# Second experts without GpSimd: VectorE makes every lower half, and the weight sums of the second product end one step earlier

## The chip, the cores and the metric

One core of one Trainium2 chip runs the whole program. The metric is device time in microseconds (us): the median of three runs before the change is 1219.12 us (1217.57 to 1220.42).

## The reference, cut to what matters

Linear attention with a norm over each head, then a layer with a SiLU gate, then four weighted experts. The last part is what the change touches:

```python
p = domain_probs / (domain_probs.sum(-1, keepdims=True) + 1e-09)
for e in range(E):                                # N = 2304, D = 512, E = 4, F = 1024
    h = np.maximum(x @ w1[e], 0.0)
    out += p[:, e:e + 1] * (h @ w2[e])
```

## The kernel before, in words

**Number format.** Each float32 operand of a matmul is held as two rounded parts, an upper half and a lower half. `split` (L157) makes them: ScalarE copies the value into the rounded type (upper half, L159), then VectorE or GpSimd subtracts that copy from the value (lower half, L160). A product uses upper times upper, lower times upper and upper times lower, so three matmuls stand for one.

**First stage, to about 466 us.** Attention and the first layer, in an order that a table (`PROGRAM`) and a loop over units fix. Its last two units overlap with the opening of the second experts; `flush` (L831) adds their results into `acc` on VectorE, four instructions at a time (L839).

**Second experts, class `Second`, from about 466 us to the end.** The 2304 tokens are three tiles of 768 tokens (two halves of 384 each; the short words of the change call a tile a pair of halves). The four experts are taken as eight halves of 512 hidden columns. So there are 24 steps, step n being expert half n mod 8 on tile n div 8. In a step the first product (`first`, L256) takes seven sub-products of twelve matmuls, built from sums and differences of quarter blocks: with weights a11, a12, s2, s1, s3, s4, a22 and inputs b11, b21, t2, t1, t3, b22, t4. The results go through `keep` (ScalarE), `add` and `relu` (VectorE), become c11, c12, c22, c21, and `oph` splits them into hidden operands. The second product reads those: in the eight steps of tile 0 by `second` (L313, plain blocks, eight groups of twelve matmuls), in tiles 1 and 2 by `again` (L338, the seven sub-products, with hidden sums t1 to t4 from `sumh`). `gather` adds each result into `acc` on VectorE (L310).

**Weights.** In tile 0 the weights are loaded (`load1`, `load2`), split (`op1`, `op2`) and written split to DRAM (`put_away`, L218); tiles 1 and 2 read them back (`get`, L223). The sums s1 to s4 of the second product's weights are needed from step 8 on. They are made by VectorE (`sumw`, L202) in a loop of their own over the eight expert halves, split by `op2` and put away. `opx` splits the inputs of a tile (seven per tile), `sumx` (L233) makes t1 to t4 of the inputs.

**What sets the order.** `events` (L372) gives each call a slot; one slot is one sub-product of TensorE, a step has 15 slots (14 from step 9 on), and `self.start[n]` is the first slot of step n. The calls are sorted by slot and issued in that order. Every engine, and SP's queue that issues all these DMAs, takes its own instructions strictly in that order: an instruction that waits holds back all that stand behind it on its engine. So `put_away` in SP's queue waits for the lower half that it writes, and the loads behind it wait too. Calls at negative slots (`early`) are issued among the units of the first stage, the others after its last unit.

**GpSimd's part before.** `pool` (L379) goes as the engine of the lower half to: three of seven inputs of a tile (`opx`), all seven first weights of step 0 and three of seven in steps 1 to 7 (`op1`), three of four plain second weights in steps 0 to 7 (`op2`), and of the hidden operands c22 in step 0 and in steps 8 to 23, t3 and t4 in steps 8 to 23 (`oph`).

**PSUM.** Two accumulators per product, x and z, lie in two banks that swap roles each step (`bank`, L166). TensorE may write a bank again when `keep`, `add`, `relu` or `gather` has read it.

Of the kernel before, what the change touches and what calls it, by code (L numbers as in the profile page):

```python
# [80 lines left out]
class Second:  # L81
# [290 lines left out]
    def events(self):  # L372
# [3 lines left out]
        def put(slot, f, *a):  # L376
            ev.append((slot, len(ev), f, a))

        pool = self.nc.gpsimd  # L379
        for n in range(self.steps):  # L380
            t, q = divmod(n, E2)
            b0, after = self.start[n], self.start[n + 1]
            make = t == 0

            if q == 0:
                start_of_last = self.start[max(n - 1, 0)]
                at = [start_of_last + k for k in (2.2, 4, 8.2, 9.4)] + [b0 + k for k in (6.2, 3, 8.2)]

                of = {"t1": start_of_last + 7.2, "t2": start_of_last + 7.3, "t3": b0 + 5.5, "t4": b0 + 7.3}
                if t == 0:  # L390

                    at = [k - 27 for k in (0, 1, 3, 2, 5, 6, 4)]
                    of = {self.B[k]: (min(at[2:4]) - 0.2 if k == 3 else at[k] - 0.1) for k in (2, 3, 4, 6)}
                for k in range(7):
                    put(at[k], self.opx, t, k, pool if k in (1, 3, 5) and t == 0 or k in (0, 1, 5) and t else None)
                    if self.B[k][0] == "t":
                        put(of[self.B[k]], self.sumx, t, self.B[k])
                for k, name in ((3, "t1"), (6, "t2"), (6, "t4"), (4, "t3")):
                    put(max(at[2:4]) + 0.01 if k == 3 else at[k] + 0.01, self.t.pop, (t, name))

            lead = self.LEAD + (2.5, -2)[n] if n < 2 else self.LEAD
            for k in range(7):
                i = b0 + 1 + 2 * k
                put(i, self.first, n, k)
                if q == E2 - 1:
                    put(i + 0.01, self.x.pop, (t, k))
                if not make:
                    put(i - self.LEAD, self.get, n, 1, k)
                    continue
                if k == 2:  # L410
                    put(i - lead - (1.8 if n != 1 else 0.2), self.sumw, n, 1, "s1")
                    put(i - lead - (1.7 if n != 1 else 0.1), self.sumw, n, 1, "s2")
                if k in (4, 5):
                    put(i - lead - 1.7, self.sumw, n, 1, "s3" if k == 4 else "s4")
                put(i - lead, self.op1, n, k, pool if k in (1, 4, 6) or n == 0 else None)
                put(i - lead + 2, self.put_away, n, 1, k)
            if make:
                for k, (i, j) in enumerate(((1, 0), (1, 1), (0, 0), (0, 1))):
                    put(b0 - (self.LEAD + 5 if n else 35) + 0.5 * k, self.load1, n, i, j)
                for k, name in ((4, "a11"), (4, "a21"), (5, "a12"), (6, "a22"), (3, "s1"), (4, "s3"), (5, "s2"), (5, "s4")):  # L420
                    put(b0 + 1.01 + 2 * k - lead, self.raw.pop, (n, 1, name))
            put(b0 + 2.1, self.keep, n, "x", "c11")
            put(b0 + 4.1, self.add, n, "z", "c11")
            put(b0 + 6.1, self.keep, n, "x", "c12")
            put(b0 + 8.1, self.keep, n, "z", "c22")
            put(b0 + 10.1, self.add, n, "x", "c22")
            put(b0 + 12.1, self.add, n, "z", "c12")
            put(b0 + 12.2, self.ps.pop, (n, "z"))

            put(b0 + 4.3, self.relu, n, "c11")  # L430
            put(b0 + (5.3 if n else 6.15), self.oph, n, "c11")
            put(b0 + 10.3, self.relu, n, "c22")
            put(b0 + 10.5, self.oph, n, "c22", None if make and n else pool)
            put(b0 + 12.25, self.relu, n, "c12")
            put(b0 + 14.05, self.relu, n, "c21")
            put(b0 + 14.06, self.ps.pop, (n, "x"))
            if make:
                put(b0 + 12.5, self.oph, n, "c12")
                put(b0 + 14.1, self.oph, n, "c21")
                for i, name in ((5.4 if n else 6.2, "c11"), (12.6, "c22"), (12.6, "c12"), (14.2, "c21")):  # L440
                    put(b0 + i, self.f.pop, (n, name))

                for k, (i, j) in enumerate(((0, 0), (0, 1), (1, 0), (1, 1))):
                    at = b0 + ((7.2, 8.6, 10.2, 14.7) if n else (7.2, 8.6, 15.2, 17.7))[k]
                    put(at - 5.5, self.load2, n, i, j)
                    put(at, self.op2, n, f"a{i + 1}{j + 1}", pool if k != 1 else None)
                    put(at + 0.01, self.raw.pop, (n, 2, f"a{i + 1}{j + 1}"))
                    if k != 2:
                        put(at + 2.5, self.put_away, n, 2, (0, 1, None, 6)[k])
                for b in range(4):  # L450
                    for d in range(2):
                        put(after + 4 * b + 2 * d, self.second, n, b, d)
                    put(after + 4 * b + 3.2, self.gather, n, b, *self.BLOCKS[b])
                    put(after + 4 * b + 3.21, self.ps.pop, (n, b))
                for i in range(2):
                    for j in range(2):
                        put(after + (10.1, 14.1)[1 - j], self.h.pop, (n, f"b{i + 1}{j + 1}"))
                        put(after + (6.1, 14.1)[i], self.w2.pop, (n, f"a{i + 1}{j + 1}"))
            else:
                put(b0 + 12.3, self.sumh, n, "t1")  # L460
                put(b0 + 12.31, self.f.pop, (n, "c12"))
                put(b0 + 12.4, self.oph, n, "t1")
                put(b0 + 12.5, self.sumh, n, "t2")
                put(b0 + 12.51, self.f.pop, (n, "c22"))
                put(b0 + 12.52, self.f.pop, (n, "t1"))
                put(after + 1.11, self.oph, n, "t2")
                put(after + 1.12, self.sumh, n, "t3")
                put(after + 1.13, self.f.pop, (n, "c11"))
                put(after + 1.14, self.oph, n, "t3", pool)
                put(after + 1.15, self.f.pop, (n, "t3"))  # L470

                u = after + (1 if n < self.steps - 1 else 3)
                put(u + 0.16, self.sumh, n, "t4")
                put(u + 0.17, self.f.pop, (n, "t2"))
                put(after + 5.5, self.oph, n, "t4", pool)
                put(after + 5.51, self.f.pop, (n, "t4"))
                put(after + 3.3, self.oph, n, "c21")
                put(after + 3.31, self.f.pop, (n, "c21"))
                for m, k in enumerate(self.ORDER):
                    put(after + 2 * m, self.again, n, k)  # L480
                    put(after + 2 * m - self.LEAD, self.get, n, 2, k)
                for m, g in enumerate(self.GATHER):
                    last = n == self.steps - 1
                    if last and m == 6:
                        for d in range(2):
                            put(after + 2 * m + 0.45, self.gather, n, *g, d)
                    else:
                        put(after + 2 * m + (1.1 if m < 6 else 0.45), self.gather, n, *g)
                put(after + 11.2, self.ps.pop, (n, "oz"))
                put(after + 12.46, self.ps.pop, (n, "ox"))  # L490
            if n == E2:
                put(b0 + 2.0, self.change)
            if q % 2 == 0:
                put(b0 - 8 if n else 0, self.load_p, t, q // 2)
            else:
                put(b0 + 14.06, self.pb.pop, (t, q // 2))
            if n == self.steps - 1:
                parts = ((9.5, 1, 0), (11.5, 1, 1), (13, 0, 0), (16, 0, 1, (0,)), (16, 0, 1, (1,)))
                for b, (slot, j, i, *ds) in enumerate(parts):
                    put(after + slot, self.leave_last, j, i, b, *ds)  # L500
            elif q == E2 - 1:
                for k in range(PW // 256):
                    put(self.start[n + 3 + k] + 11.5, self.leave, n + 2 + k, t, 2 * k)

        for n in range(E2):
            a, b = self.start[2 * n] + (7 if n == 0 else 0), self.start[2 * n + 1] + (3 if n == 0 else 0)
            for k, (i, j) in enumerate(((1, 0), (1, 1), (0, 0), (0, 1))):
                put(a + 0.4 + 0.1 * k, self.load2, n, i, j, True)
            for at, name in ((a, "s1"), (a + 2, "s2"), (b, "s3"), (b + 2, "s4")):
# [467 lines left out]
```

## Time and profile before

| what | value |
|---|---|
| runs | 1217.57, 1219.12, 1220.42 us |
| the profiled execution | 1215.1 us, of which 1213.2 us are the span of the core |
| TensorE matmul busy | 1178.1 us (97%) |
| VectorE busy | 838.1 us (69%) |
| ScalarE busy | 459.7 us (38%) |
| GpSimd busy | 312.5 us (26%) |
| chain that ended last | TensorE 83%, VectorE 2%, ScalarE 1% of the span |

The profile's numbers are of one execution; its 1215.1 us are 4.0 us under the median of the runs. TensorE is called PE, VectorE DVE, ScalarE ACT, GpSimd POOL and SyncE SP in the rows. A row of the timeline is an instruction or several equal ones, with its start, its length, and in brackets how long its engine was idle before it and what released it. Busy time says where an engine worked, the idle time of TensorE what can be won.

### The profile page before, as it was taken

The numbers are of one execution on the slowest core, as the hardware profiler recorded it, in microseconds if no ns is written. First come the engines' busy times: TensorE is split into PE (matmuls) and PEld (weight loads), VectorE is DVE, ScalarE is ACT, GpSimd is POOL, SyncE is SP. The second block draws the span as 40 slices with busy tenths as digits, with TensorE's granted clock in tenths as the row PEclk, the third lists the DMA queues.
The fourth block names the chain that finished last, engine by engine and source line by source line (L and its number), as shares of the span: only waits on it lengthen the run. The fifth ranks groups of instructions, "written<-read, shape, count | busy, mean of one in ns | idle before, by whom it ended". The sixth has DMA issues, their size and how long they took to land.

```text
span 1213.2 us, 17113 instructions
## 1 busy us (share of the span) xinstructions
PE 1178.1 (97%) x6513; PEld 1105.0 (91%) x6513; DVE 838.1 (69%) x1081; ACT 459.7 (38%) x726; POOL 312.5 (26%) x220
## 2 busy tenths in 40 slices
PE   6899999999999999999999999999999899999997
PEld 5777798888888889999999999999999899999997
DVE  4986554655564456877777867788888876666775
ACT  4555543343333243544444433333333332333222
POOL 3553442311310013522222311111113211111112
PEclk9999999999999999999999999999999999999999
DMA  9613121200200007799878677999998878888763
GB/s 327 216 57 114 35 70 35 71 18 1 97 27 1 1 1 238 274 358 323 315 271 309 237 281 281 317 308 338 307 323 285 290 241 249 277 266 277 248 203 120
DMA packets 94854, 242.91 MB, mean 200 GB/s; under 512 B 11244, under 2 KB 42420, under 8 KB 94772
## 3 DMA queue, kind: packets, MB, share of 16 engines
q1 hardware_dynamic: 92756, 238.63, 57.9%
q10 hardware_dynamic: 2016, 3.18, 0.7%
q8 instruction: 52, 0.85, 0.3%
q14 instruction: 30, 0.25, 0.1%
HBM read 178.30 MB, written 63.48 MB: 199 GB/s over the span
## 4 chain that ended last, share of the span: by engine, by line
PE 83%; DVE 2%; issue 1%; ACT 1%; DMA 0%; DVEq 0%; ACTq 0%
PE ps_x L251 16%; PE a L827 13%; PE p_h L789 12%; PE ps_z L251 12%; PE ps_o L332 11%; PE ps_ox L251 10%; PE ps_oz L251 8%; DVE f L286 0%; PE ps_t L350 0%; DVE f L269 0%; DMA w<-w_dram 0%; DVE s L202 0%; DVE t L292 0%; DVE acc L310 0%; ACT hid L159 0%
## 5 line engine op out<-in xcount | busy, mean ns | idle before, releaser
L251 PE MATMUL ps_x<-x,w 128*128 128x384 f32 x1152 | 215.8, 335 | 1.9 <-ACT x L159 1.9
L251 PEld LDWEIGHTS ps_x<-x,w 128*128 128x128 f32 x1152 | 201.4, 188 | 2.3 <-ACT x L159 2.2
L251 PE MATMUL ps_z<-x,w 128*128 128x384 f32 x864 | 163.6, 337 | 2.1 <-DVE f L286 2.1
L251 PEld LDWEIGHTS ps_z<-x,w 128*128 128x128 f32 x864 | 152.4, 189 | 2.9 <-DVE f L286 2.5
L159 ACT ACTIVATE hid<-f 128x768 fp32r<-128x768 f32 x80 | 67.6, 845 | 211.3 <-DVE f L286 211.3
L251 PE MATMUL ps_ox<-hid,w 128*128 128x384 f32 x768 | 145.0, 337 | 2.1 <-issue 2.1
L332 PE MATMUL ps_o<-hid,w 128*128 128x384 f32 x768 | 142.7, 335 | 0.0
L251 PEld LDWEIGHTS ps_ox<-hid,w 128*128 128x128 f32 x768 | 134.1, 188 | 2.7 <-issue 2.7
L332 PEld LDWEIGHTS ps_o<-hid,w 128*128 128x128 f32 x768 | 134.3, 188 | 0.1
L789 PE MATMUL p_h<-x_hi,w_hi 128*128 128x512 f32 (+1 forms) x320 | 119.7, 374 | 1.1 <-ACT o L725 1.1
L160 POOL TENSOR_TENSOR hid<-t,hid 128x768 fp32r<-128x768 f32 x32 | 61.0, 1906 | 231.0 <-ACT hid L159 226.1
L804 DVE TENSOR_TENSOR sg<-p_h,sg 128x512 f32<-128x512 f32 (+1 forms) x80 | 50.7, 636 | 99.9 <-ACT sg L803 99.6
L789 PE MATMUL p_h<-x_lo,w_hi 128*128 128x512 f32 (+1 forms) x320 | 119.1, 372 | 0.5 <-DVE x_lo L775 0.5
L827 PE MATMUL a<-h_lo,w_hi 128*128 128x512 f32 (+1 forms) x320 | 118.3, 370 | 1.1 <-DVE h_lo L813 1.1
L789 PE MATMUL p_h<-x_hi,w_lo 128*128 128x512 f32 (+1 forms) x320 | 119.2, 373 | 0.0
L827 PE MATMUL a<-h_hi,w_hi 128*128 128x512 f32 (+1 forms) x320 | 118.5, 370 | 0.0
L827 PE MATMUL a<-h_hi,w_lo 128*128 128x512 f32 (+1 forms) x320 | 118.0, 369 | 0.0
L251 PE MATMUL ps_oz<-hid,w 128*128 128x384 f32 x576 | 108.2, 335 | 1.7 <-issue 1.4
L251 PEld LDWEIGHTS ps_oz<-hid,w 128*128 128x128 f32 x576 | 100.5, 188 | 2.6 <-issue 2.0
L159 ACT ACTIVATE hid<-t 128x768 fp32r<-128x768 f32 x64 | 54.0, 843 | 125.2 <-DVE t L292 125.2
L803 ACT ACTIVATE sg<-p_h 128x512 f32<-128x512 f32 (+1 forms) x80 | 44.4, 555 | 146.7 <-PE p_h L789 139.3
L160 POOL TENSOR_TENSOR w<-raw,w 128x512 fp32r<-128x512 f32 x41 | 59.2, 1451 | 153.2 <-ACT w L159 69.5
(133 smaller groups left out, 1824.5 us busy)
## 6 DMA issues: line engine op xcount, KB each, us to landing
w<-w_dram SPq DMA_DIRECT2D x224, 512.0 KB, 4.5
w_dram<-w SPq DMA_DIRECT2D x112, 512.0 KB, 4.9
raw<-in_w SPq DMA_DIRECT2D x192, 128.0 KB, 3.5
wd_raw<-in_wd SPq DMA_DIRECT2D x28, 512.0 KB, 3.8
pb<-p_dram SPq DMA_DIRECT2D x12, 384.0 KB, 6.0
kv_first_lo<-in_kv SPq DMA_DIRECT2D x6, 512.0 KB, 10.2
q_raw<-in_qt SPq DMA_DIRECT2D x6, 512.0 KB, 7.5
out<-o ACTq DMA_DIRECT2D x12, 256.0 KB, 4.4
```

Source lines behind the costliest of these rows:

```text
L159: self.nc.scalar.activation(t[:, 0], f, AF.Copy)
L160: (eng or self.nc.vector).tensor_tensor(t[:, 1], f, t[:, 0].bitcast(F32), op=ALU.subtract)
L251: self.nc.tensor.matmul(p[:, f, :HN], w[0][:, a, c : c + 128], x[:, b, kp, :], start=self.FRESH[k] and a == b == kp == 0, stop=b == kp == ...
L332: self.nc.tensor.matmul(self.ps[n, b][:, e, :HN], w[:, u, c : c + 128], h[:, v, kp, :], start=self.count[key] == 1, stop=self.count[key] = ...
L789: nc.tensor.matmul(p[:, :n], wt[:, 0, cols], xt[:, kc, :], start=k == 0, stop=k == 3 * KC - 1)
L803: nc.scalar.activation(sg[:, :n], p[:, :n], AF.Sigmoid)
L804: nc.vector.tensor_tensor(sg[:, :n], p[:, :n], sg[:, :n], op=ALU.mult)
L827: nc.tensor.matmul(o, a, m, start=first and k == 0, stop=last and k == 2)
```

## The change

`pool` becomes None, so that every `eng or self.nc.vector` gives VectorE. Three slots move. The `relu` of c21 in step 0 goes from slot 14.05 to 13.1, ahead of two weight sums. The lower half of c21 in the last step goes from 3.3 to 7.2 slots into the second product. And the loop that makes s1 to s4 of the second product starts its sixteen halves at equal distances, from step 0.5 to step 14.2, where it had one half in each of the steps 0 to 15 (the last beginning at slot 219, step 15; now at slot 207.8, in step 14).

```diff
-        pool = self.nc.gpsimd
+        pool = None
...
-            put(b0 + 14.05, self.relu, n, "c21")
+            put(b0 + (14.05 if n else 13.1), self.relu, n, "c21")
...
-                put(after + 3.3, self.oph, n, "c21")
-                put(after + 3.31, self.f.pop, (n, "c21"))
+                u = after + (3.3 if n < self.steps - 1 else 7.2)
+                put(u, self.oph, n, "c21")
+                put(u + 0.01, self.f.pop, (n, "c21"))
...
+        def part(h):
+            k, f = divmod(0.5 + h * 13.7 / 15, 1)
+            return self.start[int(k)] + f * (self.start[int(k) + 1] - self.start[int(k)])
+
         for n in range(E2):
-            a, b = self.start[2 * n] + (7 if n == 0 else 0), self.start[2 * n + 1] + (3 if n == 0 else 0)
+            a, b = part(2 * n), part(2 * n + 1)
```

Below this the loop is as it was: `sumw` at 5.5 slots after `a` (or 7.5, `b` alike), the split 1.8 slots and `put_away` 3.7 slots after that.

**VectorE where the first stage ends.** The four L839 (L844 in the changed file) are the last `flush`; w_4001 is the weight s4 of step 0, w_4013 its a22, w_4022 and w_4077 belong to a12 of the second product. Before, the lower halves stood on GpSimd:

```order
L202 TENSOR_TENSOR s<-raw_3605,s 128x512
L839 TENSOR_TENSOR acc<-a_3845,acc 128x512
L839 TENSOR_TENSOR acc<-a_3846,acc 128x512
L839 TENSOR_TENSOR acc<-a_3847,acc 128x512
L839 TENSOR_TENSOR acc<-a_3848,acc 128x512
L269 TENSOR_TENSOR f<-ps_z,f 128x768
L286 SCALAR_TENSOR_TENSOR f<-f,pb 128x768
L160 TENSOR_TENSOR hid<-f,hid 128x768
```

Now, on VectorE:

```order
L202 TENSOR_TENSOR s<-raw_3605,s 128x512
L844 TENSOR_TENSOR acc<-a_3845,acc 128x512
L844 TENSOR_TENSOR acc<-a_3846,acc 128x512
L844 TENSOR_TENSOR acc<-a_3847,acc 128x512
L844 TENSOR_TENSOR acc<-a_3848,acc 128x512
L160 TENSOR_TENSOR w_4001<-s,w_4001 128x512
L160 TENSOR_TENSOR w_4013<-raw_3599,w_4013 128x512
L269 TENSOR_TENSOR f<-ps_z,f 128x768
L286 SCALAR_TENSOR_TENSOR f<-f,pb 128x768
L160 TENSOR_TENSOR hid<-f,hid 128x768
L160 TENSOR_TENSOR w_4060<-raw_4004,w_4060 128x512
L160 TENSOR_TENSOR w_4077<-raw_4022,w_4077 128x512
```

The lower halves of s4 and a22 stand behind the flush and ahead of the first `add` of the second experts.

**SP's queue at the same place, in the changed kernel**, with the engines and queues whose semaphores each waits for (raw_4022 is the load of a12):

```order
L218 DMA w_dram<-w_4001 128x1024 [waits DMAHW4_49,DVE_49]
L178 DMA raw_4016<-in_w 128x256 [waits DMAHW5_49]
L178 DMA raw_4016<-in_w 128x256 [waits DMAHW6_49]
L178 DMA raw_4019<-in_w 128x256 [waits DMAHW7_49]
L178 DMA raw_4019<-in_w 128x256 [waits DMAHW0_49]
L185 DMA raw_4022<-in_w 128x256 [waits DMAHW1_49]
L185 DMA raw_4022<-in_w 128x256 [waits DMAHW2_49]
```

The order of the queue is as before; where this `put_away` waited for POOL, it now waits for DVE.

**VectorE in the last step, in the changed kernel** (step 23; the L310 are gathers of the second product):

```order
L310 TENSOR_TENSOR acc<-ps_ox,acc 128x2x384
L160 TENSOR_TENSOR hid<-t,hid 128x768
L292 TENSOR_TENSOR t<-t,f 128x768
L160 TENSOR_TENSOR hid<-t,hid 128x768
L310 TENSOR_TENSOR acc<-ps_oz,acc 128x2x384
L292 TENSOR_TENSOR t<-f,t 128x768
L310 TENSOR_TENSOR acc<-ps_ox,acc 128x2x384
L160 TENSOR_TENSOR hid<-t,hid 128x768
L310 TENSOR_TENSOR acc<-ps_oz,acc 128x2x384
L160 TENSOR_TENSOR hid<-f,hid 128x768
L310 TENSOR_TENSOR acc<-ps_ox,acc 128x2x384
```

The lower half of t3 (second `hid<-t`) now stands right behind the sum that makes t3 and ahead of the gather from ps_oz; the lower half of c21 (`hid<-f`) has moved behind two gathers.

## Rows read from the trace of the kernel before

**Rows 1.** Profile page, part 1: busy time and share of each engine

```profile
PE 1178.1 (97%) x6513; PEld 1105.0 (91%) x6513; DVE 838.1 (69%) x1081; ACT 459.7 (38%) x726; POOL 312.5 (26%) x220
```

**Rows 2.** Timeline of PE: start us, length us, what, idle before and releaser

```profile
486.02 2.35 PE L332 MATMUL ps_o<-hid,w 128*128 128x384 f32 x12
...
494.69 3.92 PE L251 MATMUL ps_z<-x,w 128*128 128x384 f32 x12 [2.13 <-DVE f L286]
498.42 1.76 PE L332 MATMUL ps_o<-hid,w 128*128 128x384 f32 x9
...
952.86 2.32 PE L251 MATMUL ps_oz<-hid,w 128*128 128x384 f32 x12 [1.45 <-issue]
...
969.84 2.38 PE L251 MATMUL ps_x<-x,w 128*128 128x384 f32 x12 [1.86 <-ACT x L159]
...
1199.03 2.35 PE L251 MATMUL ps_ox<-hid,w 128*128 128x384 f32 x12 [1.94 <-issue]
```

**Rows 3.** Critical chain, window 522 to 526: start us, us, what

```profile
523.61 2.08 PE ps_x L251 x12
```

**Rows 4.** Windows view, 496 to 497 us: busy time of each engine, PEclk, DMA share, GB/s

```profile
496.00:497.00 1.00, 1.00 (x5) 1.00 (x4) 1.00 (x2) 1.00 (x3) 0.37 (x1) 0.50 0.00 0
```

**Rows 5.** Windows view of L160 alone, second experts: DVE busy, POOL busy, PEclk, DMA

```profile
466.00:1208.00 742.00, 156.97 (x171) 175.68 (x103) 1.00 0.82 280
```

**Rows 6.** Instructions of L160: count, duration ns min/median/max, first and last start us

```profile
L160 DVE TENSOR_TENSOR w<-s,w x53: 674/684/2283, 493.1 to 941.9; 128x512 fp32r<-128x512 f32 x53
L160 POOL TENSOR_TENSOR w<-raw,w x41: 1283/1409/2043, 454.9 to 710.3; 128x512 fp32r<-128x512 f32 x41
...
L160 POOL TENSOR_TENSOR hid<-t,hid x32: 1839/1870/2530, 746.8 to 1197.2; 128x768 fp32r<-128x768 f32 x32
```

**Rows 7.** Groups of instructions on DVE, forms apart: busy us, mean ns, idle before

```profile
L286 DVE SCALAR_TENSOR_TENSOR f<-f,pb 128x768 f32<-128x768 f32 x72 | 76.8, 1067 | 2.3
L160 DVE TENSOR_TENSOR hid<-f,hid 128x768 fp32r<-128x768 f32 x63 | 69.1, 1096 | 38.6 <-ACT hid L159 37.6
...
L202 DVE TENSOR_TENSOR s<-raw,raw 128x512 f32<-128x512 f32 x32 | 42.7, 1337 | 0.0
```

**Rows 8.** Timeline of DVE in and after step 15

```profile
950.93 0.96 DVE L160 TENSOR_TENSOR hid<-t,hid 128x768 fp32r<-128x768 f32 x1 [0.97 <-ACT hid L159]
951.81 0.95 DVE L310 TENSOR_TENSOR acc<-ps_ox,acc 128x768 f32<-128x768 f32 x1
...
966.30 2.60 DVE L233 TENSOR_TENSOR t<-acc 128x768 f32<-128x768 f32 x1
```

**Rows 9.** Timeline of POOL, 966 to 968 us

```profile
966.21 1.88 POOL L160 TENSOR_TENSOR hid<-t,hid 128x768 fp32r<-128x768 f32 x1 [4.43 <-ACT hid L159]
```

**Rows 10.** Timeline of DVE, end of first stage and step 0

```profile
473.74 2.75 DVE L839 TENSOR_TENSOR acc<-a,acc 128x512 f32<-128x512 f32 x4 [4.60 <-PE a L827]
...
488.91 2.38 DVE L202 TENSOR_TENSOR s<-raw,raw 128x512 f32<-128x512 f32 x2
...
493.68 0.95 DVE L286 SCALAR_TENSOR_TENSOR f<-ps_x,pb 128x768 f32<-128x768 f32 x1
```

**Rows 11.** Timeline of POOL, the lower half of s4 of step 0

```profile
469.93 1.28 POOL L160 TENSOR_TENSOR w<-s,w 128x512 fp32r<-128x512 f32 x1 [1.34 <-ACT w L159]
```

**Rows 12.** Timeline of SP's queue: put_away of s4, then the loads of a12

```profile
471.35 0.38 SPq L218 DMA_DIRECT2D w_dram<-w  x1
...
474.31 0.90 SPq L185 DMA_DIRECT2D raw<-in_w  x2
```

**Rows 13.** Instructions on tile raw, 465 to 500 us: issue to landing

```profile
DMA to landing us min/median/max: 2.6/3.5/4.7
```

**Rows 14.** Timeline of ACT: the upper half of a12

```profile
480.69 0.62 ACT L159 ACTIVATE w<-raw 128x512 fp32r<-128x512 f32 x1
```

**Rows 15.** Timeline of DVE, last step: the lower half of c21

```profile
1195.54 2.52 DVE L160 TENSOR_TENSOR hid<-f,hid 128x768 fp32r<-128x768 f32 x1
```

**Rows 16.** Windows view, steps 8 to 15 by time: busy of PE, PEld, DVE, ACT, POOL

```profile
749.00:950.00 201.00, 201.00 (x1167) 200.89 (x1166) 167.44 (x175) 68.35 (x91) 41.49 (x22) 1.00 0.90 310
```

## The prediction

> **What bounds the kernel now.** I read the page's first part, then TensorE's timeline for its idle time, then VectorE's and SP's around each gap. TensorE is busy for 97% of the span [rows 1], so only its waits can be won, and only a new wait of TensorE can cost. In the second experts it goes from one sub-product of 2.08 us [rows 3] to the next, with three places where it does not [rows 2]:
> - The opening, step 0: idle for 2.13 us before 494.69, until VectorE's relu of c21, which frees the bank. Then one sub-product takes 3.73 us (494.69 to 498.42), 1.65 us over 2.08, at a granted clock of 0.50, which is the lower of the two levels [rows 4]. Together 3.8 us.
> - Steps 15 and 16: 1.45 us before 952.86 and 1.86 us before 969.84.
> - The last step: 1.94 us before 1199.03.
>
> That is 9 us in all, the most that this change can give back.
>
> Two more things are to be seen. VectorE is slower while GpSimd works: the difference at 966.30 took 2.60 us [rows 8] beside a GpSimd instruction from 966.21 to 968.09 [rows 9], so some 0.8 us of work came after that one's end; the lower half at 1195.54 took 2.52 us [rows 15] where an undisturbed one takes 0.96 [rows 8]. And such a stretched instruction stands ahead of each of the three places: the two sums of 2.38 us together at 488.91 ahead of the relu at 493.68 [rows 10], and the two just named.
>
> **The change part by part.**
>
> *110 subtractions leave GpSimd.* 103 lie in the second experts and take 175.68 us there [rows 5]; seven belong to operands made earlier. By the code 58 work on 768 elements (17 c22, 32 t3 and t4, 9 inputs) and 52 on 512 (28 first weights, 24 second). On GpSimd one costs 1.87 or 1.41 us [rows 6], on VectorE 0.96 [rows 8] or 0.68 [rows 6]: 58 x 0.96 + 52 x 0.68 = 91 us. What VectorE gets back from no longer running beside GpSimd, from the three groups that are most above 0.96 and 0.68 [rows 7]: 63 x 0.14 + 72 x 0.11 + 32 x 0.66 = 38 us. So VectorE does some 53 us more in 742. In tile 1 it worked 167 of 201 us [rows 16]; three more instructions a step are 2.9 us in 29, less what comes back, so about 90%. TensorE hides this wherever VectorE is not late, and I put these steps at 0.
>
> The Trainium skill (Perfetto Trace Analysis, section Optimizing Scalar/DVE Operations) says that when VectorE is saturated, giving work to ScalarE or even GpSimd can make sense, but that GpSimd and VectorE share a port to SBUF, so that moving work between these two might not help. By its first half this change would give the time of rival B below; the trace speaks for its second half, with 2.60 us beside 0.96 and a VectorE at 167 of 201 us.
>
> The order counts more than the share, because VectorE now waits for ScalarE's copy between an operand and its lower half, 0.97 us each [rows 8], with nothing placed between for c22 and t3. The narrowest step of tile 0 is step 3: between the add of c22 and the upper half of c12 stand three more weight instructions of 0.6 us (0.68 less the 0.08 by which 951.81 starts before 950.93 + 0.96 is over [rows 8]). VectorE's list from that add to that upper half comes to 10.5 us, counted along the new order, where TensorE gives five slots, 10.4, and the lower half is late by 0.4 more: +0.5 us, bounds 0 and 1.
>
> *The opening.* The relu of c21 moves ahead of two sums, and the stretched sums are undisturbed: the old 2.13 us go. But two other things come. First, the lower half of s4 was made by GpSimd at 469.93 [rows 11], while VectorE stood idle for 4.60 us before its last flush [rows 10]. On VectorE it stands behind the flush, which runs until 476.5 because it waits for TensorE: it ends at 477.1. SP's queue holds its put_away, which started at 471.35 [rows 12] and now starts at 477.1, 5.75 us later, and behind it every load of the opening. The second load of a12 (two from 474.31, 0.90 us) is then issued at 480.5 instead of 474.8 and lands 3.5 us later [rows 13], at 484.0; ScalarE could have copied it at 480.69 [rows 14]. Second, VectorE's list from there: copy 0.62 [rows 14], lower halves of a12 and of the next a11 2 x 0.6, add of c22 and relu 1.95 (the second waits for the first), and ScalarE's copy within the 0.97, so the upper half of c22 is there at 488.7, and TensorE, due at 486.02, idles 2.7 us. Then the lower half of c22 0.87, one weight 0.6, add and relu of c12 1.95, copy: c12 at 493.0, another wait of 2.9 us after the eight matmuls that c22 allows. Four matmuls (0.7) and three sub-products (3 x 2.08) later it is 499.9 where before it was 498.42: **+1.5 us**. What becomes late next, the add of step 1's c11, ends about 1 us before its bank is wanted. Bounds: loads that land 2.6 us after issue give +0.6; were a12 in time, VectorE's list alone gives 497.6, -0.8; if the clock falls after both waits, twice 1.65 more, though the first fall would pass within the second wait: +3.1 with one.
>
> *Steps 15 and 16.* The sums s3 and s4 of the last expert half and their splits (4 x 0.6 = 2.4 us) leave step 15. In come five instructions in step 15 (c22, t3, t4 and two input splits, 5 x 0.87 = 4.4 us at the spacing of 950.93 to 951.81 [rows 8]) and two waits of 0.97. So VectorE has about 4 us more of its own, and gets back what it was stretched by. Counted instruction by instruction from the start of step 15, its gather frees the bank of slot 235 (now at 952.86) 1.3 us late instead of 1.45, the copy of t3 is 0.9 late instead of 1.86, a gather between them 0.45, and one in step 17 about 1.0. I take -0.3; bounds -3.3 (both waits gone) and +1.5 (half a wait more at each).
>
> *The last step.* The lower half of c21 (2.52) no longer stands ahead of the gather that TensorE waits for at 1199.03. But t3's lower half, which GpSimd made, does, with its wait for the copy: the gather from ps_oz, next after it, ends about 2.4 us later than before (at 1197.05), and TensorE waits there instead. The sub-product of 1199.03 starts at 1199.2: +0.2 us. Bounds -1.9 (the wait gone) and +1.9 (0.2, and 1.65 if the clock falls as after the 2.13 us: the waits of 1.45 to 1.94 us left no such sub-product [rows 2], 2.4 us is nearer to 2.13).
>
> *What costs nothing.* The lower halves among the first stage's last units (seven, 6 us) are covered by VectorE's idle time there, 4.60 us before the flush alone; if that cover were gone, the SiLU of the first stage would be late. GpSimd's own end releases nothing else. After the opening the put_aways in tile 0 wait for VectorE instead of GpSimd, and the loads queued behind them run at least 5.5 slots (11 us) ahead of use. The sixteen halves of the weight sums take their loads and put_aways with them in SP's queue; the last put_away goes from slot 230 to 219, and its read-back stays at 231, so this wait only shrinks.
>
> **The sum.** +0.5 + 1.5 - 0.3 + 0.2 = +1.9 us on the profiled 1215.1, so 1217.0; that execution is 4.0 us under the median, so against the runs 1219.1 + 1.9 = **1221.0 us**. 0.2% is 2.4 us, about what a measurement of this kernel can tell from no change.
>
> **The rivals.**
>
> *A. The gaps close (faster, 0.26).* If the loads of the opening do not decide and VectorE, undisturbed, keeps ahead, the opening gives -0.8 to -3.8, steps 15 and 16 up to -3.3, the end up to -1.9. About half of the 9 us: 1214.6. For it: an instruction that was stretched by GpSimd stands ahead of each gap. Against: s4 stands behind a flush that waits for TensorE itself, and each gap gets a new instruction at the same place.
>
> *B. VectorE becomes the bound (slower, 0.18).* In steps 8 to 14 its list is 25 instructions of 0.87 us, some 4.4 weight instructions of 0.6 and three waits of 0.97 for a copy: 27.3 us of the step's 29.2. It decides from 1.9 us more, one wait for SP's loads or two copies that come late. Half a microsecond to one in each of seven steps: +3.5 to +7, so with the sum about 1226. Against: in the changed list the tightest gather of a normal step still ends 0.5 us before its bank is wanted.
>
> *C. The clock (slower, 0.16).* The forecast's waits of 2.4 to 2.9 us are longer than the one after which the clock fell. A fall at both, 1.65 us each and not covered: 1221.0 + 3.3 = 1224.3.
>
> That the change does not do what it says is excluded: GpSimd's list ends with the first stage.
>
> **How the numbers follow.** The forecast, within 0.2% of no change, gets 0.40, the rivals A 0.26, B 0.18 and C 0.16. Faster is A, 0.26; slower is B and C, 0.34; same 0.40. The range reaches half into A and past C, leaving about 0.1 on either side: 1214.5 to 1225. The likeliest case's own range is 1217 to 1221.5.
>
> **What would show it.** Right: GpSimd empty after the first stage; VectorE's busy time near 890 us; its sums raw from raw near 0.7 us; SP's put_away of s4 some 5 us later and, at step 0's second product, two waits of TensorE instead of one; at the end the wait moved from ps_ox to ps_oz. Wrong: no wait at the opening (A), or waits in every step of tile 1 (B).

## The result, and the profile after

The changed kernel takes **1231.69 us** (median of three runs, 1230.85 to 1234.39) against 1219.12 before: ratio 1.0115, 95% interval 1.0100 to 1.0131. It is 12.6 us slower; 1221.0 was forecast, 1225.0 was the range's upper end. The profiled execution took 1231.69 us too, with a span of 1229.8.

The profile page after, parts 1, 4 and 5 (columns as in [rows 1] and [rows 7]):

```profile
PE 1187.3 (97%) x6513; PEld 1108.5 (90%) x6513; DVE 869.5 (71%) x1191; ACT 458.5 (37%) x726; POOL 125.7 (10%) x110
...
PE 70%; DVE 10%; DMA 2%; ACT 2%; issue 1%; SPq 0%; ACTq 0%; DVEq 0%
...
L160 DVE TENSOR_TENSOR hid<-f,hid 128x768 fp32r<-128x768 f32 x80 | 76.5, 956 | 37.6 <-ACT hid L159 36.4
```

VectorE makes 110 instructions more and is busy for only 31 us more than in [rows 1]: the same lower half takes 956 ns in the mean, not 1096 [rows 7]. VectorE is not full at 71%. Yet its share of the chain that ended last went from 2 to 10%, so something on it is late, and TensorE's waits say for whom. The view of waits after, engine PE, 430 to 1230 us (engine, what, line, releaser: us in all, times, longest):

```profile
PE ps_t L350 <- DVE acc L310: 5.1, 6, 1.3
PE ps_oz L251 <- DVE acc L310: 2.4, 2, 2.2
PE ps_oz L251 <- issue: 2.3, 3, 1.2
PE ps_x L251 <- DVE f L269: 1.9, 1, 1.9
PE ps_o L332 <- ACT hid L159: 1.0, 2, 0.9
PE ps_z L251 <- DVE f L269: 1.0, 2, 0.7
PE a L832 <- DVE acc L844: 0.9, 1, 0.9
PE ps_x L251 <- ACT x L159: 0.7, 1, 0.7
```

L350 is new: the transposes of finished output blocks in `leave`, which the kernel calls at slot 11.5 of steps 10, 11, 12, 18, 19 and 20. To size each place I took the start of the same product in both traces; the growth of the difference is what the stretch lost:

| stretch, up to | before, us | after, us | lost |
|---|---|---|---|
| first product of step 0 | 465.88 | 470.87 | 5.0 |
| the opening, up to the product behind its last wait in either trace | 498.42 | 505.27 | 1.9 |
| ends of steps 1 to 4, first product of step 5 | 617.19 | 626.20 | 2.2 |
| steps 5 to 12, all at the transposes of steps 10 to 12 | 855.23 | 867.73 | 3.5 |
| steps 15 to 17 | 984.75 | 998.22 | 1.0 |
| transposes of steps 18 to 20 | 1095.80 | 1112.16 | 2.9 |
| last step, last transposes but one | 1206.75 | 1223.31 | 0.2 |

Of the first 5.0 us only 1.2 belong to the change: the starts from the wait at L832 on come 1.2 us later, 0.9 us of it idle. The other 3.8 us are there from 110 us on, ahead of all that the change touches: TensorE had its lower clock early in this execution and not in the profiled one before, whose time was 4.0 us under its median. Windows view (start:end, length, busy us of PE, PEld, DVE, ACT, POOL, then PEclk, DMA share, GB/s), after:

```profile
25.00:30.00 5.00, 4.31 (x21) 4.34 (x22) 3.60 (x6) 1.94 (x3) 1.27 (x1) 0.50 1.06 379
...
95.00:100.00 5.00, 3.81 (x14) 3.33 (x15) 4.78 (x7) 2.99 (x5) 1.42 (x2) 0.66 0.10 39
```

and before:

```profile
25.00:30.00 5.00, 4.45 (x33) 3.76 (x33) 5.00 (x9) 3.66 (x7) 1.27 (x1) 1.00 1.06 374
...
95.00:100.00 5.00, 5.00 (x34) 4.49 (x34) 3.39 (x4) 1.48 (x3) 1.29 (x1) 1.00 0.18 46
```

In the profiles of the ten kernels below the first product of step 0 starts anywhere from 467.0 to 471.7, with or without GpSimd. So the change's own terms are 1.2 + 1.9 + 2.2 + 3.5 + 1.0 + 2.9 + 0.2 = 12.9 us in this pair of executions; the medians differ by 12.6. That they meet so closely is partly luck: the opening and steps 1 to 4, where the kernels of 3 and 4 below run the same instructions, lost 3.3 and 0.8 us in the profile of 3, and 4.0 and 1.4 in that of 4.

**Where the 6.4 us at the transposes come from.** VectorE, ScalarE and TensorE in step 10, after:

```profile
800.39 0.96 DVE L286 SCALAR_TENSOR_TENSOR f<-f,pb 128x768 f32<-128x768 f32 x1
...
801.45 0.85 ACT L159 ACTIVATE hid<-f 128x768 fp32r<-128x768 f32 x1 [5.47 <-DVE f L286]
802.33 0.96 DVE L160 TENSOR_TENSOR hid<-f,hid 128x768 fp32r<-128x768 f32 x1 [0.97 <-ACT hid L159]
803.20 0.95 DVE L310 TENSOR_TENSOR acc<-ps_oz,acc 128x768 f32<-128x768 f32 x1
...
804.21 1.09 PE L350 MATMUL ps_t<-ident,acc 128*128 128x128 f32 x8 [0.75 <-DVE acc L310]
```

The same place before:

```profile
791.31 0.96 DVE L286 SCALAR_TENSOR_TENSOR f<-f,pb 128x768 f32<-128x768 f32 x1
...
792.40 0.96 DVE L310 TENSOR_TENSOR acc<-ps_oz,acc 128x768 f32<-128x768 f32 x1
793.29 1.83 POOL L160 TENSOR_TENSOR hid<-f,hid 128x768 fp32r<-128x768 f32 x1 [9.51 <-ACT hid L159]
794.29 1.04 PE L350 MATMUL ps_t<-ident,acc 128*128 128x128 f32 x8
```

Before, the gather (L310) follows the relu (L286) at once and ends 0.9 us before the transposes want its bank. After, the lower half of c22 stands between them. Its work is 0.87 us, but it first waits 0.97 us for ScalarE's copy, and VectorE, with the gather ready behind, does nothing. The two together, 1.84 us, less the 0.9 us in hand, make the transposes start 0.9 us late, 0.75 us of it idle. In most other steps that bank is wanted later.

The Trainium skill (TensorE: Matmul & The Clock Gate, section "Architectural detail: the array is 16× 32×32, not 1× 128×128") states that ScalarE's and VectorE's queues are strictly first in, first out. The trace agrees: 0.97 us idle with a ready gather behind.

### The profile page after: what moved, and what is told of

It is laid out like the page before. It is cut to its first block, busy times and chain, and to the rows that moved or that the text cites. A ratio compares the mean times of both kernels' runs of the same rounds, so it can differ in the third digit from the quotient of the medians.

```text
span 1229.8 us, 16963 instructions
## 1 busy us (share of the span) xinstructions
PE 1187.3 (97%) x6513; PEld 1108.5 (90%) x6513; DVE 869.5 (71%) x1191; ACT 458.5 (37%) x726; POOL 125.7 (10%) x110
## 4 chain that ended last, share of the span: by engine, by line
PE 70%; DVE 10%; DMA 2%; ACT 2%; issue 1%; SPq 0%; ACTq 0%; DVEq 0%
PE ps_x L251 13%; PE a L832 13%; PE p_h L794 12%; PE ps_o L332 9%; PE ps_z L251 8%; PE ps_ox L251 8%; PE ps_oz L251 5%; DVE hid L160 2%; DVE f L286 2%; ACT hid L159 2%; DVE acc L310 2%; DMA raw<-in_w 2%; DVE f L269 1%; DVE t L292 1%; DVE w L160 1%
## 5 line engine op out<-in xcount | busy, mean ns | idle before, releaser
L832 PE MATMUL a<-h_hi,w_hi 128*128 128x512 f32 (+1 forms) x320 | 119.2, 372 | 0.9 <-DVE acc L844 0.9
L832 PE MATMUL a<-h_lo,w_hi 128*128 128x512 f32 (+1 forms) x320 | 118.8, 371 | 1.1 <-DVE h_lo L818 1.1
L809 DVE TENSOR_TENSOR sg<-p_h,sg 128x512 f32<-128x512 f32 (+1 forms) x80 | 50.7, 636 | 96.8 <-ACT sg L808 96.5
L832 PE MATMUL a<-h_hi,w_lo 128*128 128x512 f32 (+1 forms) x320 | 118.5, 370 | 0.0
L160 DVE TENSOR_TENSOR hid<-f,hid 128x768 fp32r<-128x768 f32 x80 | 76.5, 956 | 37.6 <-ACT hid L159 36.4
L160 DVE TENSOR_TENSOR hid<-t,hid 128x768 fp32r<-128x768 f32 x64 | 61.1, 955 | 34.8 <-ACT hid L159 34.6
```

Source lines behind the costliest of these rows:

```text
L160: (eng or self.nc.vector).tensor_tensor(t[:, 1], f, t[:, 0].bitcast(F32), op=ALU.subtract)
L809: nc.vector.tensor_tensor(sg[:, :n], p[:, :n], sg[:, :n], op=ALU.mult)
L832: nc.tensor.matmul(o, a, m, start=first and k == 0, stop=last and k == 2)
```

## The experiments

Each ran beside the kernel before on the same chip. They ran in three groups (1 to 3 and 6; 4, 5, 7 and 8; 9 and 10), beside which the kernel before took 1219.34, 1220.41 and 1218.84 us, and the changed kernel ran in none of them. So a difference in us across groups carries up to 1.6 us of that; a ratio is always to the kernel before in the same group. **Queue theory**: what costs is not the amount of work that VectorE got but a few lower halves that stand in its queue, or a store in SyncE's, ahead of something TensorE needs. **Rivals**: VectorE has too much to do; or the moved slots lose it.

**1 and 2. The change in its two parts.** First the engine alone, in the kernel before:

```diff
-        pool = self.nc.gpsimd
+        pool = None
```

> Edit: the kernel before, with every lower half of the second experts on VectorE, and no slot moved. Queue theory (each lost microsecond is a lower half that stands in VectorE's queue ahead of an instruction which frees a bank, or completes a unit, for the next product; the changed kernel's trace gives 0.9 us in the first stage, 1.9 at the opening, 2.2 at the ends of steps 0 to 4, 6.4 at the six pairs of transposes of finished blocks, 1.0 in steps 13 to 16, 0.2 in the last step): the transposes' 6.4, the first stage's 0.9 and the opening's 1.9 or more stay, what the spread weight sums add at the ends of steps 0 to 4 goes: 1229.3 us, between 1227.5 and 1231; TensorE still waits some 5 us for VectorE's gathers ahead of the transposes. Rival (VectorE simply has too much work, and the moves relieve it): 1232 us or more, with the waits at the ends of the steps grown as well. A second rival (the moved slots are the loss): 1220 us.

Then the slots alone: the changed kernel with the reverse of that edit.

> Edit: the changed kernel with GpSimd making the same 110 lower halves as in the kernel before; only the moved slots remain (c21 of the first step, c21 of the last, the spread weight sums). Queue theory: no wait of TensorE at the transposes of finished blocks, none for the last accumulation of the first stage; what is left is at most the 2.2 us at the ends of steps 0 to 4: 1220 us, between 1218.5 and 1221.5. Rival (the moved slots are the loss): 1227 us or more.

The engine alone: 1231.19 us, ratio 1.0100 (1.0079 to 1.0121), just above the range given. The slots alone: **1216.28 us, 0.9976 (0.9961 to 0.9990)**, a gain of some 3 us, below the range given; neither theory had it. The loss is the engine's, the slots are not to blame. The profile of the slots alone shows 2.1 us of their gain at the end: the wait of 1.94 us at the last step [rows 2] is gone, since the lower half of c21 no longer stands ahead of the gather. With VectorE making t3 it is lost again there (4 below). By the profiles that makes 1.7 of the 3.8 us by which the two parts (11.9 less 3.1 us) fall short of the change's 12.6; the rest was not followed up.

**3. One lower half put behind the gather**, with ScalarE's copy that it follows, in tiles 1 and 2 of the changed kernel:

```diff
-            put(b0 + 10.5, self.oph, n, "c22", None if make and n else pool)
+            put(b0 + (10.5 if make else 11.15), self.oph, n, "c22", None if make and n else pool)
```

> Edit: in tiles 1 and 2 alone the halves of the hidden unit c22 are recorded at slot 11.15 of a step and not at 10.5, that is behind the gather of slot 11.1 and not ahead of it; everything else is the changed kernel. Queue theory: TensorE's six waits of 0.75 to 1.3 us for that gather, ahead of the transposes of finished blocks, vanish, 5.1 us and what they bring with them, 6.4 us in all: 1225.3 us, between 1224.3 and 1226.5. Rival (VectorE is too full, whatever the order): the wait moves to the next instruction that VectorE owes, and the time stays above 1229 us.

1222.73 us, 1.0029 (1.0015 to 1.0043): 9.0 us less than the changed kernel, with the same work on VectorE (870.5 us). All six waits are gone. VectorE and TensorE in step 10 of this kernel:

```profile
797.08 0.96 DVE L286 SCALAR_TENSOR_TENSOR f<-f,pb 128x768 f32<-128x768 f32 x1
...
798.10 0.96 DVE L310 TENSOR_TENSOR acc<-ps_oz,acc 128x768 f32<-128x768 f32 x1
...
799.01 0.96 DVE L160 TENSOR_TENSOR hid<-f,hid 128x768 fp32r<-128x768 f32 x1
...
799.99 1.03 PE L350 MATMUL ps_t<-ident,acc 128*128 128x128 f32 x8
```

While the gather runs, ScalarE finishes the copy: VectorE does not wait at all. From step 5 to step 12 this kernel loses nothing on the kernel before. The 2.6 us beyond the six waits are in steps 15 to 17 (the expectations call this stretch steps 13 to 16), where the same instruction stood ahead of other gathers: this kernel gains 1.7 us there on the kernel before, where the changed one loses 1.0.

**4. The same in the last step**, on top of 3: t3's halves behind the gather that the 2.2 us wait is for.

```diff
-                put(after + 1.14, self.oph, n, "t3", pool)
-                put(after + 1.15, self.f.pop, (n, "t3"))
+                u = after + (1.14 if n < self.steps - 1 else 3.13)
+                put(u, self.oph, n, "t3", pool)
+                put(u + 0.01, self.f.pop, (n, "t3"))
```

> Edit: the kernel of e3_c22_behind_gather, and in the last step the halves of the hidden sum t3 are recorded at slot 3.13 of the last product and not at 1.14, that is behind the gather of slot 3.1. Queue theory: TensorE's wait of 2.2 us for that gather in the last step goes, as the six at the transposes did: 1220.6 us, between 1219.3 and 1221.9. Rival (at the end VectorE has simply more to do than the products cover): the wait moves to the next gather, 1222.7 us.

1220.57 us, 1.0003 (0.9991 to 1.0015), as the queue theory said; the wait of 2.2 us is gone.

**5. The one instruction in the kernel before**: only the lower half of c22 in tiles 1 and 2 goes to VectorE.

```diff
-            put(b0 + 10.5, self.oph, n, "c22", None if make and n else pool)
+            put(b0 + 10.5, self.oph, n, "c22", None if n else pool)
```

> Edit: the kernel before with one thing changed: in tiles 1 and 2 the lower half of c22, 16 of the 110 halves, goes from GpSimd to VectorE, at its old slot 10.5. Queue theory: these 16 alone bring the six waits at the transposes of finished blocks, 5 to 6.4 us, and something in steps 13 to 16: 1225.3 us, between 1223.8 and 1227.5. Rival (the loss follows the amount of work that VectorE gets): 16/110 of the 11.9 us that all halves cost, 1221 us.

1228.45 us, 1.0076 (1.0055 to 1.0097): these 16 of 110 halves bring 8.0 us, more than the range given, since steps 15 to 17 cost more than I put in. The view of waits, engine PE, 440 to 1230 us, of this kernel:

```profile
PE ps_t L350 <- DVE acc L310: 4.3, 6, 0.7
PE ps_oz L251 <- issue: 2.5, 3, 1.2
...
PE ps_ox L251 <- DVE acc L310: 1.4, 1, 1.4
```

**6 and 7. The opening.** First GpSimd makes the opening's lower halves again (a second name, `early`, for GpSimd; from step 1 on VectorE makes all). Of the calls only the arguments are shown:

```diff
-        pool = None
+        pool, early = None, self.nc.gpsimd
-  self.opx, t, k, pool if k in (1, 3, 5) and t == 0 or k in (0, 1, 5) and t else None
+  self.opx, t, k, early if k in (1, 3, 5) and t == 0 else pool if k in (0, 1, 5) and t else None
-  self.op1, n, k, pool if k in (1, 4, 6) or n == 0 else None
+  self.op1, n, k, early if n == 0 else pool if k in (1, 4, 6) else None
-  self.oph, n, "c22", None if make and n else pool
+  self.oph, n, "c22", early if n == 0 else None if make else pool
-  self.op2, n, f"a{i + 1}{j + 1}", pool if k != 1 else None
+  self.op2, n, f"a{i + 1}{j + 1}", early if n == 0 and k != 1 else None
```

> Edit: the changed kernel, but GpSimd makes the lower halves of the opening again (three of the split inputs of tile 0, those of the first weights of step 0, of the second weights of step 0, and c22 of step 0); from step 1 on VectorE makes all. Queue theory: the 0.9 us wait of the first stage's last accumulation and the 1.9 us of the opening come back, the rest stays: 1228.9 us, between 1227.9 and 1230; the transposes still wait some 5 us. Rival (the opening's loss comes from the c21 that was moved to slot 13.1 and from the sums, not from the lower halves): 1231 us or more.

Then, in the changed kernel, one store of step 0 behind two loads in SyncE's queue:

```diff
-                put(i - lead + 2, self.put_away, n, 1, k)
+                put(i - lead + (2.7 if n == 0 and k == 5 else 2), self.put_away, n, 1, k)
```

> Edit: the changed kernel with one DMA moved in SyncE's queue: in step 0 the storing of the weight sum s4 comes behind the two loads of a12 and not ahead of them. Theory of the prediction (the store waits for VectorE and holds the loads behind it, and so the lower halves that need them): the loads are issued some 2 us earlier, TensorE's two waits at the opening (1.9 and 0.9 us) shrink, 1230.2 us, between 1229.2 and 1231.2. Rival (VectorE's own queue makes the opening late, the loads would be in time): 1231.7 us and the two waits as they were.

GpSimd in the opening: 1228.99 us, 1.0077 (1.0054 to 1.0099), as expected in size; the wait at L832 is gone. But its opening still lost 1.0 us of the 1.9, in one long wait for c12's upper half, a wait that the kernel before does not have:

```profile
494.10 1.19 PE L332 MATMUL ps_o<-hid,w 128*128 128x384 f32 x4 [3.18 <-ACT hid L159]
```

More of what it saves is in steps 1 to 4, which lost 0.8 us here and not 2.2.

The one store: 1228.58 us, 1.0074 (1.0053 to 1.0094), 3.1 us less than the changed kernel where 1.5 were expected. By the ratios, 1.0115 and 1.0074, it is 5.0 us, and the two intervals leave some 3 us either way: the gain is clear, its size is not. The opening of the changed kernel (SPq is SyncE's queue):

```profile
481.39 0.68 DVE L160 TENSOR_TENSOR w<-s,w 128x512 fp32r<-128x512 f32 x1
...
482.10 0.33 SPq L218 DMA_DIRECT2D w_dram<-w  x1
...
484.79 0.90 SPq L185 DMA_DIRECT2D raw<-in_w  x2
...
489.13 1.15 ACT L159 ACTIVATE w<-raw 128x512 fp32r<-128x512 f32 x2 [2.32 <-DMA raw<-in_w]
...
492.02 3.74 PE L251 MATMUL ps_x<-x,w 128*128 128x384 f32 x12 [1.89 <-DVE f L269]
...
498.21 0.97 PE L332 MATMUL ps_o<-hid,w 128*128 128x384 f32 x4 [0.88 <-ACT hid L159]
```

and with the store moved (its first product of step 0 starts 0.8 us later, at 471.66):

```profile
478.13 0.90 SPq L185 DMA_DIRECT2D raw<-in_w  x2
...
482.90 0.33 SPq L218 DMA_DIRECT2D w_dram<-w  x1
...
487.49 1.15 ACT L159 ACTIVATE w<-raw 128x512 fp32r<-128x512 f32 x2
...
490.74 2.24 PE L251 MATMUL ps_x<-x,w 128*128 128x384 f32 x12
...
496.56 0.97 PE L332 MATMUL ps_o<-hid,w 128*128 128x384 f32 x4 [2.19 <-ACT hid L159]
```

The loads leave 6.7 us earlier, ScalarE no longer waits for them, the wait of 1.89 us is gone, and with it the sub-product of 3.74 us. The next wait has grown from 0.88 to 2.19 us: it is for c12, at the end of VectorE's own list, and the loads do not decide it. From 465.88 to 498.42, times of the kernel before, this kernel loses nothing on that kernel: it gains 0.6 us, and the kernel before has a sub-product at the lower clock there (3.73 us) where this one has none.

**8. Which halves cost nothing.** The kernel of 2, and the six lower halves of the inputs of tiles 1 and 2 go to VectorE:

```diff
-  pool if k in (1, 3, 5) and t == 0 or k in (0, 1, 5) and t else None
+  pool if k in (1, 3, 5) and t == 0 else None
```

> Edit: the kernel of e2_moves_alone (GpSimd kept, the slots moved), and the lower halves of the split inputs of tiles 1 and 2, 6 in all, go to VectorE. Queue theory: no gather stands behind these, and TensorE's wait for the split inputs of tile 1's end, 1.9 us in e2_moves_alone and 0.7 in the kernels where VectorE makes them, shrinks to 0.7: 1215.1 us, between 1213.8 and 1216.5. Rival (every half that VectorE gets costs): 1216.9 us or more.

**1215.18 us, 0.9963 (0.9950 to 0.9976)**, the lowest median of the ten, though its interval overlaps that of 2. The wait for the split input is 1.5 us, not the 0.7 expected, so part of the reason given is not borne out. That these halves cost nothing on VectorE is borne out as far as the runs can tell.

**9 and 10. All repairs together.** The kernel of 4 with the store of 7 moved, so that GpSimd still does nothing in the second experts:

> Edit: the kernel of f1_last_t3_too with the DMA of f3_put_away_behind_loads moved as well; GpSimd still does nothing in the second experts. Queue theory: the repairs add up, 1220.6 less the 3.1 us that f3_put_away_behind_loads gained: 1217.5 us, between 1216.3 and 1219, no slower than the kernel before although VectorE makes all 110 halves. Rival (an idle GpSimd itself costs, whatever the order): 1220 us or more.

and the kernel of 4 with GpSimd in the opening, as in 6:

> Edit: the kernel of f1_last_t3_too with GpSimd making the lower halves of the opening, as in e4_opening_on_gpsimd. Queue theory: 1220.6 less the 2.7 us of e4_opening_on_gpsimd: 1217.9 us, between 1216.7 and 1219.2, about what moving the one DMA gives. Rival (GpSimd's share of the opening is worth more than the DMA's place): 1216.5 us or less.

1217.85 us, 0.9993 (0.9982 to 1.0004), and 1216.66 us, 0.9986 (0.9975 to 0.9997). The first has all 110 halves on VectorE (870.5 us busy) and is no slower than the kernel before: an idle GpSimd costs nothing of itself. The second is between its two theories.

The Trainium skill (Perfetto Trace Analysis, section Optimizing Scalar/DVE Operations) expects that moving work between GpSimd and VectorE might not help, as they share a port. The mended kernel agrees: 0.9993, with the order put right.

## Why the prediction was wrong, step by step

- **"TensorE hides this wherever VectorE is not late, and I put these steps at 0": the step that failed.** I had seen the wait of 0.97 us, "with nothing placed between for c22 and t3", but judged it by the normal step, whose "tightest gather ... still ends 0.5 us before its bank is wanted". Six steps are not normal: in them the transposes of `leave` want a gather's bank at slot 11.5. They measured 6.4 us instead of 0, of the 10.7 us by which the forecast was short; with c22 behind the gather they are gone (3), and c22 alone brings them (5).
- **Rival B** had about the price (+3.5 to +7) and the wrong mechanism: VectorE was not the bound of steps 8 to 14, since the same work in another order cost nothing.
- **"The lower halves among the first stage's last units cost nothing"** failed by 1.2 us. The cover was looked for ahead of the flush (4.60 us, [rows 10]); these halves are issued earlier. Timeline of DVE, then of PE, after:

```profile
457.67 0.96 DVE L160 TENSOR_TENSOR x<-acc,x 128x768 fp32r<-128x768 f32 x1
458.55 1.29 DVE L160 TENSOR_TENSOR w<-raw,w 128x512 fp32r<-128x512 f32 x2
459.75 0.68 DVE L809 TENSOR_TENSOR sg<-p_h,sg 128x512 f32<-128x512 f32 x1
...
461.74 2.48 DVE L844 TENSOR_TENSOR acc<-a,acc 128x512 f32<-128x512 f32 x4
```

```profile
462.57 0.47 PE L832 MATMUL a<-h_hi,w_hi 128*128 128x512 f32 x1 [0.89 <-DVE acc L844]
```

  and the timeline of DVE before:

```profile
454.55 0.69 DVE L804 TENSOR_TENSOR sg<-p_h,sg 128x512 f32<-128x512 f32 x1 [1.57 <-ACT sg L803]
```

  Three halves of 2.2 us stand where VectorE had been idle for 1.57 us. What I had named as late if the cover were gone, the first stage's SiLU (L804, now L809), did come late: 5.2 us after its time before, 3.8 of which this execution was behind anyway. The accumulation that TensorE waits for came late with it.
- **The opening, +1.5: right** in mechanism, and in this execution nearly in size: 1.9. The store of s4 went at 482.10, 10.75 us later than in [rows 12], of which 5.0 are this execution's late start: 5.75 were forecast. There were two waits as forecast, of 1.89 and 0.88 us where I had counted 2.7 and 2.9, and a short one before them (0.74) that I had not seen. The size is not fixed: the kernels of 3 and 4, with the same opening, lost 3.3 and 4.0 us. Timeline of PE in 4, where the waits are near those counted and the lower clock comes after the second (3.01 and not 2.25 us for the product behind it):

```profile
488.93 2.35 PE L251 MATMUL ps_x<-x,w 128*128 128x384 f32 x12 [2.63 <-DVE f L269]
...
495.14 1.65 PE L332 MATMUL ps_o<-hid,w 128*128 128x384 f32 x4 [2.46 <-ACT hid L159]
496.58 3.01 PE L251 MATMUL ps_x<-x,w 128*128 128x384 f32 x12
```

  Experiment 7 shows that the store caused the first of the two waits, and not the second. The bound of -0.8 that I gave for loads in time was close: -0.6.
- **"The narrowest step of tile 0 is step 3", +0.5**: step 3's end lost 0.6, as counted. Two other ends, of steps 1 and 4, lost 0.7 each in this execution. The six other profiles with both parts of the change show 0.8 to 1.5 us for these steps together, not 2.2; those with one part 0.3 to 0.9, and the kernel of 5, whose tile 0 is that of the kernel before, 0.6. So a part of the 2.2 is the spread of one execution to the next; which instructions make the rest was not tried.
- **Steps 15 and 16, -0.3**: the sum was wrong by itself, as the four waits counted, set against the two of before, make +0.3 (-0.15 + 0.45 - 0.96 + 1.0). They came out nearly as counted: 1.25 us (1.3 forecast), 0.27 (0.45), 0.72 (0.9) and, in step 17, 0.93 (1.0). But the first half of the same list, in step 15, lost 1.1 in three places where my count had shown no wait, and the stretch came to +1.0. The lower half of c22 counts here too: with it behind the gathers the stretch is at -1.7 (3).
- **The last step, +0.2: right.** The wait moved from one gather to the next, now 2.18 us for t3's. Timeline of DVE and PE, after:

```profile
1211.64 0.96 DVE L160 TENSOR_TENSOR hid<-t,hid 128x768 fp32r<-128x768 f32 x1 [0.99 <-ACT hid L159]
1212.51 0.95 DVE L310 TENSOR_TENSOR acc<-ps_oz,acc 128x768 f32<-128x768 f32 x1
...
1213.52 2.36 PE L251 MATMUL ps_oz<-hid,w 128*128 128x384 f32 x12 [2.18 <-DVE acc L310]
```

- **The clock (rival C)** did not decide here: one sub-product of 3.74 us in the opening, as in the kernel before. It could have cost more: in the profiles of 3 and 6 TensorE had its lower clock (granted 0.50) in the last step as well, behind the same wait of 2.2 us.
- Of the signs, VectorE's busy time was 869.5 us and not 890: I had counted 38 us that VectorE gets back, from three stretched groups, and it got back some 60 (838.1 + 91 - 869.5).

## What to carry to other kernels

Before an instruction is moved to another engine's queue, list what stands behind it there, and add the time that it will wait for its own input to the time that it takes; a follower of another engine's copy belongs behind the next instruction that is ready, not right behind its producer. Do this for the steps that differ from the rest, too: half of the loss sat in six steps of 24, and an engine's mean load of 71% said nothing of it. The same holds for a DMA queue: one store that waits held loads that were ready.

## What was unexpected of the hardware

The clock does not follow from the length of a wait alone. With the slots alone (2) and in the fastest kernel (8), TensorE waits at the same product for nearly the same time. Timeline of PE, in 2:

```profile
504.78 3.75 PE L251 MATMUL ps_x<-x,w 128*128 128x384 f32 x12 [2.63 <-ACT f L264]
```

and in 8:

```profile
501.46 2.39 PE L251 MATMUL ps_x<-x,w 128*128 128x384 f32 x12 [2.62 <-ACT f L264]
```

The windows view gives a granted clock of 0.54 in 2, near the lower of the two levels, and of 1.00 in 8, over the three microseconds in which this product mostly runs:

```profile
506.00:509.00 3.00, 3.00 (x11) 3.00 (x11) 2.97 (x3) 2.19 (x4) 2.87 (x2) 0.54 0.93 314
```

```profile
503.00:506.00 3.00, 3.00 (x19) 3.00 (x19) 2.97 (x3) 2.20 (x5) 2.58 (x2) 1.00 0.97 341
```

A shorter wait can be enough. In 2 the clock fell a second time, to 0.50, behind a wait of 1.86 us, as long as the one in [rows 2] that left no slow product:

```profile
975.32 3.36 PE L251 MATMUL ps_x<-x,w 128*128 128x384 f32 x12 [1.86 <-ACT x L159]
```

What else decides is open. So my price for a fall, 1.65 us after a wait of over 2 us, is a chance and not a certainty, and waits of 1.45 to 1.94 us are not safe from it.
